# Strided sparse attention and a spectral mixer on one core: the last mode split by rows, the last Z in two tiles, the first U behind V

## The chip, the cores and the metric

The kernel runs on one core of a Trainium2 chip. The metric is the device time of one execution in microseconds (us), smaller is better. Runs of the same kernel differ by a few tenths of a per cent, so a time is a median of several.

## What is computed

Two stages follow each other, and nothing between them leaves the chip.

- Attention over q, k, v of shape (8 batches, 8 heads, 576 positions, 64): heads 0 to 3 look at the last 32 positions, heads 4 to 7 at the earlier positions of the same remainder modulo 32. The result x has 8 x 576 rows of 512.
- A spectral mixer: a Fourier transform of x along the positions, its first 64 modes multiplied by one complex 512 x 512 matrix each (w_r, w_i), the inverse transform y, then u = x + y and out = u + relu(u @ w_ch).

```python
X = np.fft.rfft(x, axis=1)
Xr, Xi = np.real(X[:, :64]), np.imag(X[:, :64])
Yr = einsum('bmd,mde->bme', Xr, w_r) - einsum('bmd,mde->bme', Xi, w_i)
Yi = einsum('bmd,mde->bme', Xr, w_i) + einsum('bmd,mde->bme', Xi, w_r)
u = x + np.fft.irfft(Y, n=576, axis=1)
return u + np.maximum(u @ w_ch, 0.0)
```

The mode matrices are 134 MB in float32. They are read once, turned into float16 on the way into SBUF.

## The kernel before, in words

**Order of the work.** The order of every engine's instructions is the order in which the program writes them (a manual schedule). Each engine works through its own list, and an instruction waits by semaphores for the tiles that it reads or overwrites. An instruction that waits holds up all that stands behind it on its engine.

**Stages.** Attention for the strided heads, then for the local heads, then what must be done with x before the inverse transform. Beside all of it the mode matrices stream in (w_fetch, from L157) and are multiplied (mode, from L614). The loads are issued on the POOL queue. A tile holds two modes, real part in partitions 0 to 63, imaginary part in 64 to 127. Most loads bring two modes (512 KB in float16); the last four modes are loaded one by one, two loads of 256 KB each (the list `single`, L189 and L190). A mode is needed for two halves of the 512 input columns; the second half of the modes 48 to 63 comes last (`rest`, L1036).

**The last modes.** For the second half, modes from 48 on are multiplied with the weights as the stationary operand: 16 small matmuls (L630), 4 output blocks e by 4 input chunks c, each with 16 columns moving. Eight modes share one PSUM tile y (L624). When the tile's modes are done, VectorE adds them to what the first half gave (spectrum, L563) and puts the sum into YT. In the last group that happens after mode 61 (six modes) and after mode 63 (two modes), both in the same y tile.

**V and U.** Since u @ w_ch and u are both linear in x and y, the kernel keeps for each block of 128 output rows a V part (x @ w_ch, what the relu will see) and a U part (x), and adds to both what the modes bring. Groups of 16 modes are added to the kept parts as soon as they are there (renew, L948; matmuls at L956 and L760; ScalarE writes V back at L251, VectorE adds U at L961). Only the last group of 16 modes is left for the end. For it the spectra are turned into Z = YT @ w_ch (spec_z, from L733, copied by ScalarE into zz) and YT turned around (transposes at L1051, copied by VectorE into yy at L1053). There are two sets of each, for batches 0 to 3 and 4 to 7.

**The output items.** 18 items of two blocks follow. For item k, v_early (L984) puts the kept V into a PSUM pair with an identity matmul (L987), new_rows (L994) adds the last modes' part from zz (L1001), ScalarE makes the relu (v_done, L1013); u_early (L989) and new_rows do the same for U from yy (L992, L1001); VectorE adds both (u_done, L1020) and SyncE stores (L1028). The loop (L1065) is one item deep: V of item k stands ahead of U of item k - 1. At k = 8 the second Z is computed into a tile `held` and copied by ScalarE, ahead of V 8.

**PSUM.** Eight banks: a pool p of three pairs (six banks), handed out in turn, and two y tiles. After mode 63 the y pool is closed; its two banks hold zp and yp, and after them the pair u.

**The end before the change**, in PE's order: mode 61; the last renew; mode 62; V 0, V 1, U 0 (the identity matmuls, into three p pairs); mode 63; Z; eight transposes; V rows of 0 and 1; U rows of 0; U 1 and its rows; then the loop.

Of the kernel before, what the change touches and what calls it, by code (L numbers as in the profile page):

```python
# [10 lines left out]
FP = mybir.dt.float32  # L11
# [5 lines left out]
S = 576  # L17
# [39 lines left out]
def kernel(  # L57
# [99 lines left out]
    def w_fetch(n=1):  # L157
        for _ in range(n):
            i = len(w_tiles)
            if i >= 2 * NM:  # L160
                return
            half, m = ORDER[i]
            if i // 2 in GUEST:
                wt = big.tile([128, 2, 4, DM], F16, tag=GUEST[i // 2], name="wt")
            else:
                wt = pw.tile([128, 2, 4, DM], F16, tag="w", name="wt")
            single = []
            for ri, src in enumerate((moe_w_r, moe_w_i)):
                dst = wt[ds(64 * ri, 64)]
                rows = src[m : m + 2, ds(256 * half, 256), :].rearrange(  # L170
                    "m (p c) e -> p m (c e)", c=4
                )
                dst = dst.rearrange("p m c e -> p m (c e)")


                ones = range(2)
                if ri and not m:
                    ones = [1]
                elif i in UNEVEN and not ri:
                    a = 0  # L180
                    for n in UNEVEN[i]:
                        nc.gpsimd.dma_start(dst[a : a + n], rows[a : a + n])
                        a += n
                    continue
                elif i < 2 * NM - 4:
                    nc.gpsimd.dma_start(dst, rows)  # L186
                    continue
                single += [(j, ri, dst[:, j], rows[:, j]) for j in ones]
            for _, _, to, rows in sorted(single, key=lambda x: x[:2]):  # L189
                nc.gpsimd.dma_start(to, rows)  # L190
            w_tiles.extend((wt[:, 0], wt[:, 1]))

# [57 lines left out]
    def act_copy(out, in_):  # L250
        nc.scalar.activation(out=out, in_=in_, func=ACTF.Copy)  # L251
# [362 lines left out]
    def mode(slot, m):  # L614
# [5 lines left out]
                mode_pair(slot, m - 1)  # L620
            return
        mi, mg = m % 8, m // 8
        if mi == 0:
            ypt[slot] = psum("y")  # L624
        yp = ypt[slot]
        yv = yp.rearrange("p (m e x) -> p m e x", m=8, e=4)
        wt = w_tiles[ORDER.index((half, m))]
        for e in range(4):
            for c in range(4):
                nc.tensor.matmul(  # L630
                    yv[:, mi, e, :],
                    wt[:, XC[c], ds(128 * e, 128)],
                    Xh[half][:, c, :, :, m],
                    start=(c == 0),
                    stop=(c == 3),
                )
        if m % 2:
            w_fetch()
        ends = {5: 6, 7: 2} if mg == 7 else {7: 8}
# [294 lines left out]
        if m >= 16 and m % 16 in (2, 4):  # L934
            spec(m // 16 - 1, m % 16 // 2 - 1)

    psum_pools(p=3)
    yctx = ctx.enter_context(ExitStack())
    pss["y"] = yctx.enter_context(tc.tile_pool(name="ps_y2", bufs=2, space=PSUM))

    def spec_late(mm, kept, eng):
        up = psum("p", pair=True)
        for bq in range(2):
            mm(2, bq, up[:, bq])
        for b in range(B):
            eng(kept[b][64:96], up[ds(32 * (b % 4), 32), b // 4])

    def renew(b, ts):  # L948
# [2 lines left out]
            v0, xo = v0s[b][:, ts[0] : ts[0] + 2], xos[b][:, ts[0] : ts[0] + 2]  # L951
        else:
            v0, xo = v0h[b // 2].unsqueeze(1), xoh[b // 2].unsqueeze(1)
        vp, up = psum("p", pair=True), psum("p", pair=True)
        for j, t in enumerate(ts):
            nc.tensor.matmul(vp[:, j], idn, v0[:, j], start=True, stop=False)  # L956
            rows_of(b, t, vp[:, j], zzs, False)
# [24 lines left out]
        return [kept[b][:, t] for b in bs] if t < 4 else [half[b // 2] for b in bs[::2]]  # L982

    def v_early(k):  # L984
        vps[k] = psum("p", pair=True)
        for j, r in enumerate(own(items[k], v0s, v0h)):
            nc.tensor.matmul(vps[k][:, j], idn, r, start=True, stop=False)  # L987

    def u_early(k):  # L989
        ups[k] = psum(("p", "u")[k % 2], pair=True)  # L990
        for j, r in enumerate(own(items[k], xos, xoh)):
            nc.tensor.matmul(ups[k][:, j], idn, r, start=True, stop=False)  # L992

    def new_rows(k, acc, spectra):  # L994
        bs, t = items[k]
# [38 lines left out]

    flush()
    rest = [(0, m) for m in range(SPLIT1, NM)] + [(1, m) for m in range(SPLIT0, NM)]  # L1036
    late[22] = [lambda: v_early(0), lambda: v_early(1), lambda: u_early(0)]
    for i, (slot, m) in enumerate(rest):
        mode(slot, m)
        for w in late.get(i, ()):  # L1040
            w()
    yctx.close()
    with tc.tile_pool(name="ps_s", bufs=1, space=PSUM) as pss["s"]:
        zp = pss["s"].tile([128, 512], FP, name="zp")
        yp = pss["s"].tile([128, 2, 512], F16, name="yp")
        spec_z(3, 0, zp)
        act_copy(zzs[0], zp)
        for bq in range(2):
            for e in range(4):
                lhs = YS["YT"][:, e, 3, ds(8 * bq, 8), :].rearrange("p x m -> p (x m)")  # L1050
                nc.tensor.transpose(yp[:, bq, ds(128 * e, 128)], lhs, idn)  # L1051
        for bq in range(2):
            nc.vector.tensor_copy(out=yys[bq], in_=yp[:, bq])  # L1053
    pss["u"] = pctx.enter_context(tc.tile_pool(name="ps_u", bufs=1, space=PSUM))

    for k in range(2):
        new_rows(k, vps[k], zzs)
    for k in range(2):
        v_done(k)
    for k in range(2):  # L1060
# [3 lines left out]
        u_done(k)  # L1064
    for k in range(2, LAST + 2):  # L1065
        if k == 8:
            held = psum("p", pair=True)[:, 0]
            spec_z(3, 1, held)
            act_copy(zzs[1], held)
        if k <= LAST:  # L1070
# [42 lines left out]
```

## Time and profile before

| what | value |
|---|---|
| three runs | 427.37, 427.93, 429.17 us; median 427.93 us |
| profiled execution, its span | 426.7 us, 1.2 us under the median of the runs |
| busy share of the span: PE, VectorE, ScalarE | 81%, 55%, 51% |
| loads on the POOL queue | 81.28 MB written, 96.2% of the time of 16 DMA engines |
| mode loads of 512 KB, issue to landing | 17.7 to 18.8 us |
| last mode load issued | 382.31 us |
| first store issued | 396.88 us |
| last store issued | 420.18 us |

The profile shows one execution on the chip. PE is TensorE's matmul, PEld its weight load, DVE VectorE, ACT ScalarE, POOL GpSimd, SP SyncE. L630 is line 630 of the kernel. The chain of work that ended last is followed back from the last instruction: at each step to what released it, or to the instruction before it on its engine. In the timeline, a row has its start, its duration, the engine, the line and the operation; for merged rows (x16) the duration is that of all; brackets give the idle time before it and what ended that. A matmul's duration includes its way through the array: 512 columns occupy PE for 0.216 us and end 0.38 us after their start. In rows for stretches, the columns are busy time of PE, PEld, DVE, ACT and POOL, then the clock granted to TensorE as a share of full speed, the busy share of the DMA engines and GB/s. The sum of busy time over all engines says little here; what counts is which wait ends last in the stretch around the change.

### The profile page before, as it was taken

To read this page: it belongs to the slowest core of one execution; us is meant where nothing else is said; L and a number is where in the kernel's file an instruction comes from. 1 tells how busy PE (TensorE), PEld (TensorE's weight loads), DVE (VectorE), ACT (ScalarE), POOL (GpSimd) and SP (SyncE) were. 2 spreads that over 40 slices of the span, in tenths; PEclk is the share of its full clock that TensorE was granted. 3 is DMA by queue.
4 is the path that set the end of the run, shared out by engine and by line. 5 is a ranking of instruction groups with operands and counts; after the bars stand their busy time and mean duration, and the time that the engine had idled before them with its cause. 6 is when DMAs were issued, how large, how long until landed. Compare 5 with 4: busy or idle time off the path is not lost.

```text
span 426.7 us, 9768 instructions
## 1 busy us (share of the span) xinstructions
PE 346.4 (81%) x4167; PEld 208.2 (49%) x4167; DVE 234.7 (55%) x466; ACT 218.3 (51%) x390; POOL 110.7 (26%) x196
## 2 busy tenths in 40 slices
PE   2977878769999698889768788878788867889993
PEld 2866767554656365566433344435444423445330
DVE  3788778851355154356113246746676354655884
ACT  1687678643656356556642235423442444443872
POOL 8332333322423222222222322222232222210000
PEclk9999899967999689999995889989999979989997
DMA  8999999999999999999999999999999999995698
GB/s 150 210 212 212 213 213 213 211 211 211 214 213 213 213 213 215 212 214 215 210 214 211 213 214 213 210 213 215 212 213 214 213 213 214 214 212 105 244 355 287
DMA packets 30938, 91.62 MB, mean 215 GB/s; under 512 B 4464, under 2 KB 5232, under 8 KB 30896
## 3 DMA queue, kind: packets, MB, share of 16 engines
q0 software_dynamic: 25168, 81.28, 96.2%
q1 hardware_dynamic: 4976, 9.13, 5.9%
q10 hardware_dynamic: 752, 0.61, 0.5%
q8 instruction: 32, 0.52, 0.5%
q14 instruction: 10, 0.08, 0.0%
HBM read 162.83 MB, written 9.44 MB: 404 GB/s over the span
## 4 chain that ended last, share of the span: by engine, by line
DMA 47%; PE 29%; DVE 14%; ACT 5%; issue 3%; DVEq 0%; POOL 0%; ACTq 0%; POOLq 0%
DMA wt<-in_moe_w_i_dram 38%; DMA wt<-in_moe_w_r_dram 7%; PE y L597 5%; DVE xb L241 3%; DVE kz L283 3%; PE p L987 2%; ACT X L251 2%; PE sc L532 2%; PE tp L413 2%; PE sc L459 1%; PE p L1001 1%; PE y L532 1%; PE p L760 1%; DVE yy L752 1%; DVE rec L240 1%
## 5 line engine op out<-in xcount | busy, mean ns | idle before, releaser
L597 PE MATMUL y<-wt,X 128*32 128x512 f16 (+1 forms) x448 | 70.9, 430 | 20.1 <-DMA wt<-in_moe_w_i_dram 20.1
L186 POOL DMA_DIRECT2D wt<-in_moe_w_r_dram x59 | 34.7, 588 | 126.4 <-PE y L597 56.3
L186 POOL DMA_DIRECT2D wt<-in_moe_w_i_dram x60 | 35.4, 590 | 68.3 <-DMA wt<-in_moe_w_i_dram 44.4
L597 PEld LDWEIGHTS <-X 128*32 128x32 f16 (+1 forms) x448 | 28.1, 140 | 39.4 <-DMA wt<-in_moe_w_i_dram 18.6
L727 DVE COPY xo<-tp 128x512 f16<-128x512 f16 x32 | 22.1, 691 | 36.8 <-PE tp L725 36.8
L726 ACT ACTIVATE v<-sc 128x512 f16<-128x512 f32 x32 | 19.1, 597 | 44.2 <-PE sc L717 44.2
L717 PE MATMUL sc<-w_cp,xT 128*128 128x512 f16 x128 | 36.9, 410 | 1.9 <-DVE xT L690 1.9
L489 ACT ACTIVATE PL<-sc 128x480 f16<-128x480 f32 (+1 forms) x48 | 27.0, 578 | 21.3 <-PE sc L475 21.0
L241 DVE TENSOR_TENSOR xb<-av,rec 90x256 f16<-90x256 f32 (+2 forms) x80 | 36.0, 450 | 2.8
L240 DVE RECIPROCAL rec<-av 90x4 f32<-90x4 f32 (+2 forms) x80 | 14.6, 183 | 39.3 <-PE av L504 28.2
L251 ACT ACTIVATE yr<-y 128x512 f16<-128x512 f32 x28 | 16.7, 597 | 36.8 <-PE y L597 35.6
L961 DVE TENSOR_TENSOR xo<-p,xo 128x1024 f16<-128x1024 f32 x16 | 19.6, 1225 | 21.7 <-PE p L760 21.7
L420 DVE COPY qT<-tp 128x576 f16<-128x576 f16 x16 | 11.9, 752 | 34.7 <-PE tp L413 34.7
L251 ACT ACTIVATE v<-p 128x1024 f16<-128x1024 f32 x16 | 16.4, 1023 | 23.1 <-PE p L760 23.1
L378 ACT ACTIVATE PL<-sc 90x360 f16<-90x360 f32 (+1 forms) x48 | 22.7, 490 | 7.0 <-PE sc L371 6.4
L251 ACT ACTIVATE v<-tp 128x640 f16<-128x640 f16 (+1 forms) x24 | 19.0, 807 | 11.8 <-PE tp L447 9.3
L413 PE MATMUL tp<-cI_s,ring 64*64 64x64 f16 x864 | 22.4, 197 | 2.7 <-DVE qT L420 2.4
L459 PE MATMUL sc<-cMl_s,cI_s 128*128 128x480 f16 (+1 forms) x48 | 19.4, 405 | 4.5 <-ACT PL L489 2.9
L276 PE MATMUL tp<-cI_s,ring 72*128 72x72 f16 x256 | 15.4, 207 | 8.7 <-DMA ring<-in_v_dram 7.1
L413 PEld LDWEIGHTS <-ring 64*64 64x64 f16 x864 | 17.5, 110 | 9.4 <-issue 5.4
L251 ACT ACTIVATE kz<-tp 64x360 f16<-64x360 f16 (+1 forms) x32 | 18.9, 592 | 6.2 <-PE tp L413 5.2
L1013 ACT ACTIVATE rl<-p 128x1024 f32<-128x1024 f32 (+1 forms) x19 | 18.4, 979 | 5.7 <-PE p L1001 3.1
(142 smaller groups left out, 737.9 us busy)
## 6 DMA issues: line engine op xcount, KB each, us to landing
wt<-in_moe_w_i_dram POOLq DMA_DIRECT2D x60, 512.0 KB, 18.8
wt<-in_moe_w_r_dram POOLq DMA_DIRECT2D x59, 512.0 KB, 17.7
out_dram<-osb SPq DMA_DIRECT2D x15, 512.0 KB, 3.4
ring<-in_v_dram POOLq DMA_DIRECT2D x8, 288.0 KB, 13.4
ring<-in_q_dram POOLq DMA_DIRECT2D x8, 288.0 KB, 13.6
ring<-in_k_dram POOLq DMA_DIRECT2D x8, 288.0 KB, 13.1
ring<-in_v_dram POOLq DMA_DIRECT2D x3, 512.0 KB, 14.8
ring<-in_q_dram POOLq DMA_DIRECT2D x3, 512.0 KB, 14.8
```

The lines of the kernel that those rows point to most:

```text
L186: nc.gpsimd.dma_start(dst, rows)
L241: nc.vector.tensor_tensor(out=dst, in0=val.rearrange("p h (q c) -> p h c q", c=4), in1=rec[0:n, 0:pieces] .to_broadcast((n, pieces, 64)) . ...
L251: nc.scalar.activation(out=out, in_=in_, func=ACTF.Copy)
L378: nc.scalar.activation(out=PS[0:n, ds(POFF[t], 4 * n)], in_=scp[0:n, 0 : 4 * n], func=ACTF.Exp, scale=SCALE,)
L413: nc.tensor.transpose(tp[ds(64 * hp, 64), ds(64 * i, 64)], qn[ds(64 * hp, 64), ds(64 * (9 * g + i), 64)], idn[ds(64 * hp, 64), ds(64 * hp, ...
L459: nc.tensor.matmul(scp[:, 0 : n * times].rearrange("p (h x) -> p h x", h=times), idn, mask_rows("cMl", n, times), start=True, stop=False,)
L489: nc.scalar.activation(out=dst, in_=src, func=ACTF.Exp, scale=SCALE)
L597: nc.tensor.matmul(yp[ds(a, 32), :], Xh[half][pr, c].rearrange("p b r (h m) -> p (b r h) m", h=2)[:, :, mm % 32], wt[pr, XC[c], :], start= ...
L717: nc.tensor.matmul(vp, xT[:, ch], w_chs["cp"][:, ch, :], start=(ch == 0), stop=(ch == 3),)
L726: nc.scalar.activation(out=v0, in_=vp, func=ACTF.Copy)
L727: nc.vector.tensor_copy(out=xo.rearrange("p (h q c) -> p h q c", h=2, c=4), in_=tp[:, 0:512].rearrange("p (h c q) -> p h q c", h=2, c=4),)
L961: nc.vector.tensor_tensor(out=xo, in0=up[:, 0:n], in1=xo, op=AluOp.add)
```

## The change

- The loads of mode 63 are cut in two by columns of the row (input chunks 0 and 1, then 2 and 3): four loads of 128 KB, in the order real, imaginary, real, imaginary. (w_fetch)
- Mode 62 opens a new y tile, so that modes 62 and 63 no longer share the tile of modes 56 to 61. Mode 63 begins with a matmul on a part of the constants that is zero (64 columns), then takes the eight steps on the first two chunks, two matmuls whose result is never read (warm(2), 512 columns each), then the other eight steps. (mode)
- The three p pairs get fixed names p0, p1, p2 in place of the turn (pair). Up to the last renew they go in turn. Then V takes p0 or p1 by the parity of the item (counted from where the turn ended), odd U and the unread matmuls p2, even U the pair u. `held` takes the pair of V of the same item.
- A third unread matmul stands between mode 63 and Z.
- The first Z is computed in two column halves into the two y tiles; ScalarE copies the first half, VectorE the second. The transposes go into p2 (as yp).
- U 0 no longer stands ahead of mode 63. It comes behind the V rows of items 0 and 1, in the pair u, and VectorE's copies of yp are written after it.

```diff
@@ -185,8 +185,13 @@
                 elif i < 2 * NM - 4:
                     nc.gpsimd.dma_start(dst, rows)
                     continue
-                single += [(j, ri, dst[:, j], rows[:, j]) for j in ones]
-            for _, _, to, rows in sorted(single, key=lambda x: x[:2]):
+                for j in ones:
+                    n = 2 * DM if m + j == NM - 1 else 4 * DM
+                    for a in range(0, 4 * DM, n):
+                        single.append(
+                            (j, a, ri, dst[:, j, a : a + n], rows[:, j, a : a + n])
+                        )
+            for *_, to, rows in sorted(single, key=lambda x: x[:3]):
                 nc.gpsimd.dma_start(to, rows)
             w_tiles.extend((wt[:, 0], wt[:, 1]))
 
@@ -620,20 +625,32 @@
                 mode_pair(slot, m - 1)
             return
         mi, mg = m % 8, m // 8
-        if mi == 0:
+        if mi == 0 or m == NM - 2:
             ypt[slot] = psum("y")
         yp = ypt[slot]
         yv = yp.rearrange("p (m e x) -> p m e x", m=8, e=4)
         wt = w_tiles[ORDER.index((half, m))]
-        for e in range(4):
-            for c in range(4):
-                nc.tensor.matmul(
-                    yv[:, mi, e, :],
-                    wt[:, XC[c], ds(128 * e, 128)],
-                    Xh[half][:, c, :, :, m],
-                    start=(c == 0),
-                    stop=(c == 3),
-                )
+        last = m == NM - 1
+        steps = [(e, c) for e in range(4) for c in range(4)]
+        if last:
+            steps.sort(key=lambda x: XC[x[1]] // 2)
+            nc.tensor.matmul(
+                yv[:, mi, :, :],
+                idn,
+                cs["cT"][:, S:640].rearrange("p (e x) -> p e x", e=4),
+                start=True,
+                stop=False,
+            )
+        for i, (e, c) in enumerate(steps):
+            if last and i == 8:
+                warm(2)
+            nc.tensor.matmul(
+                yv[:, mi, e, :],
+                wt[:, XC[c], ds(128 * e, 128)],
+                Xh[half][:, c, :, :, m],
+                start=(c == 0 and not last),
+                stop=(i == 15 if last else c == 3),
+            )
         if m % 2:
             w_fetch()
         ends = {5: 6, 7: 2} if mg == 7 else {7: 8}
@@ -934,12 +951,20 @@
         if m >= 16 and m % 16 in (2, 4):
             spec(m // 16 - 1, m % 16 // 2 - 1)
 
-    psum_pools(p=3)
+    psum_pools(p=1)
+    npair = [0]
+
+    def pair(n=None):
+        if n is None:
+            n = npair[0] % 3
+            npair[0] += 1
+        return pss["p"].tile([128, 2, 512], FP, tag=f"p{n}", name="p")
+
     yctx = ctx.enter_context(ExitStack())
     pss["y"] = yctx.enter_context(tc.tile_pool(name="ps_y2", bufs=2, space=PSUM))
 
     def spec_late(mm, kept, eng):
-        up = psum("p", pair=True)
+        up = pair()
         for bq in range(2):
             mm(2, bq, up[:, bq])
         for b in range(B):
@@ -951,7 +976,7 @@
             v0, xo = v0s[b][:, ts[0] : ts[0] + 2], xos[b][:, ts[0] : ts[0] + 2]
         else:
             v0, xo = v0h[b // 2].unsqueeze(1), xoh[b // 2].unsqueeze(1)
-        vp, up = psum("p", pair=True), psum("p", pair=True)
+        vp, up = pair(), pair()
         for j, t in enumerate(ts):
             nc.tensor.matmul(vp[:, j], idn, v0[:, j], start=True, stop=False)
             rows_of(b, t, vp[:, j], zzs, False)
@@ -982,14 +1007,19 @@
         return [kept[b][:, t] for b in bs] if t < 4 else [half[b // 2] for b in bs[::2]]
 
     def v_early(k):
-        vps[k] = psum("p", pair=True)
+        vps[k] = pair((npair[0] + k % 2) % 3)
         for j, r in enumerate(own(items[k], v0s, v0h)):
             nc.tensor.matmul(vps[k][:, j], idn, r, start=True, stop=False)
 
     def u_early(k):
-        ups[k] = psum(("p", "u")[k % 2], pair=True)
+        ups[k] = pair((npair[0] + 2) % 3) if k % 2 else psum("u", pair=True)
         for j, r in enumerate(own(items[k], xos, xoh)):
             nc.tensor.matmul(ups[k][:, j], idn, r, start=True, stop=False)
+
+    def warm(n):
+        spare = pair((npair[0] + 2) % 3)
+        for _ in range(n):
+            nc.tensor.matmul(spare[:, 0], idn, v0h[0], start=True, stop=True)
 
     def new_rows(k, acc, spectra):
         bs, t = items[k]
@@ -1034,27 +1064,39 @@
 
     flush()
     rest = [(0, m) for m in range(SPLIT1, NM)] + [(1, m) for m in range(SPLIT0, NM)]
-    late[22] = [lambda: v_early(0), lambda: v_early(1), lambda: u_early(0)]
+    late[22] = [lambda: v_early(0), lambda: v_early(1)]
     for i, (slot, m) in enumerate(rest):
         mode(slot, m)
         for w in late.get(i, ()):
             w()
+    warm(1)
+    last_y = YS["YT"][:, :, 3].rearrange("p e x m -> p e (x m)")
+    zp = [psum("y"), psum("y")]
+    for j in range(2):
+        for e in range(4):
+            nc.tensor.matmul(
+                zp[j][:, 0:256],
+                last_y[:, e, 0:128],
+                w_chs["n"][:, e, ds(256 * j, 256)],
+                start=(e == 0),
+                stop=(e == 3),
+            )
+    act_copy(zzs[0][:, 0:256], zp[0][:, 0:256])
+    nc.vector.tensor_copy(out=zzs[0][:, 256:512], in_=zp[1][:, 0:256])
+    yp = pss["p"].tile([128, 2, 1024], F16, tag=f"p{(npair[0] + 2) % 3}", name="yp")
+    for bq in range(2):
+        for e in range(4):
+            nc.tensor.transpose(
+                yp[:, bq, ds(128 * e, 128)], last_y[:, e, ds(128 * bq, 128)], idn
+            )
     yctx.close()
-    with tc.tile_pool(name="ps_s", bufs=1, space=PSUM) as pss["s"]:
-        zp = pss["s"].tile([128, 512], FP, name="zp")
-        yp = pss["s"].tile([128, 2, 512], F16, name="yp")
-        spec_z(3, 0, zp)
-        act_copy(zzs[0], zp)
-        for bq in range(2):
-            for e in range(4):
-                lhs = YS["YT"][:, e, 3, ds(8 * bq, 8), :].rearrange("p x m -> p (x m)")
-                nc.tensor.transpose(yp[:, bq, ds(128 * e, 128)], lhs, idn)
-        for bq in range(2):
-            nc.vector.tensor_copy(out=yys[bq], in_=yp[:, bq])
     pss["u"] = pctx.enter_context(tc.tile_pool(name="ps_u", bufs=1, space=PSUM))
 
     for k in range(2):
         new_rows(k, vps[k], zzs)
+    u_early(0)
+    for bq in range(2):
+        nc.vector.tensor_copy(out=yys[bq], in_=yp[:, bq, 0:512])
     for k in range(2):
         v_done(k)
     for k in range(2):
@@ -1064,7 +1106,7 @@
         u_done(k)
     for k in range(2, LAST + 2):
         if k == 8:
-            held = psum("p", pair=True)[:, 0]
+            held = pair((npair[0] + k % 2) % 3)[:, 0]
             spec_z(3, 1, held)
             act_copy(zzs[1], held)
         if k <= LAST:
```

## The prediction

> **What bounds the kernel now.** I read the chain of work that ended last first, then the timeline of its last 40 us, then stretches of a tenth of a microsecond around the last weights. Up to 377 us the chain is weight loads, one behind the other, with a DMA share above 1. From 377.2 us on TensorE (PE) has more queued than the loads hold back, so the rest of the span is a queue of PE passes with a few waits in it. All that the change touches lies there. The chain (start, duration, both in us):
>
> ```profile
> 388.80 0.50 DVE xo L961
> 389.30 0.64 issue
> 389.94 0.56 DVE YT L563
> 390.54 0.64 PE y L630 x16
> 391.17 0.86 PE p L987 x4
> 392.04 0.43 PE p L992 x2
> 392.47 0.49 PE y L630 x16
> 392.98 0.30 DVE YT L563
> 393.33 1.05 PE zp L736 x4
> 394.45 0.61 ACT zz L251
> 395.10 0.45 PE p L1001 x4
> 395.55 1.07 ACT rl L1013 x2
> 396.67 0.59 PE p L987 x2
> ...
> 404.18 1.01 ACT rl L1013
> 405.23 0.59 PE p L987 x2
> ```
>
> Mode 62 (L630, 390.54) waits for VectorE's add at L563, which stood behind the 1.23 us add of L961. Then four V passes, two U passes, mode 63, its add, Z (L736), ScalarE's copy, the V rows (L1001), the relu. From 396.67 the output items follow every 1.295 us (six streams of 512 columns at 0.216 us on PE), broken once: at 404.18 PE waits for a relu (item 7) before V of item 8. The timeline there (start, duration, engine, line, operation):
>
> ```profile
> 404.05 1.04 PE L736 MATMUL p<-w_ch,YT 128*128 128x512 f16 x4
> 404.16 1.02 ACT L1013 ACTIVATE rl<-p 128x1024 f32<-128x1024 f32 x1 [0.27 <-PE p L1001]
> 405.13 0.60 ACT L251 ACTIVATE zz<-p 128x512 f16<-128x512 f32 x1
> ```
>
> ScalarE takes the relu and only then copies the second Z (405.13 to 405.73). That order decides a cost below. The last weights (stretch, its length, PE, PEld, DVE, ACT, POOL, granted clock, DMA share, GB/s):
>
> ```profile
> 391.30:391.40 0.10, 0.10 (x2) 0.03 (x1) 0.00 (x0) 0.00 (x0) 0.00 (x0) 1.00 0.20 41
> 391.60:391.70 0.10, 0.10 (x3) 0.04 (x1) 0.00 (x0) 0.00 (x0) 0.00 (x0) 1.00 0.01 0
> ```
>
> The last data packet is at 391.4 and what follows at 391.6 is a sliver, the completion: mode 63's weights are there at about 391.65, while PE came to mode 63 at 392.3. So the loads do not set the end; PE's queue does.
>
> **The change, part by part.**
>
> 1. Mode 62 gets its own y tile, and its wait for L563 goes. PE's last pass before it starts at 389.62 and mode 62's first weight load at 389.93, 0.31 later. The same form shows the same 0.31 at 381.10 to 381.41, so this is PE's own pace and not a late load. Mode 62 can start at 389.97 instead of 390.54: **-0.57**. Late next would be its own weights: by the landing above, less two loads of 1.2 us, they are there at about 389.2 (an estimate). Bounds: 0 if they land at 390.5, 0.6 at best. V's buffers are read by L961 until 390.03 and by ScalarE until 390.43; V comes at 390.44 and 390.87, so nothing new waits.
>
> 2. Between the V passes and mode 63 the two U passes go (-0.43). In come one 64-column pass on zeros (16 small passes take 0.48, so 0.03) and, after eight of the 16 steps, two unread passes of 512 columns (+0.43): **+0.03**. PE then comes to the second half of mode 63 at 389.97 + 0.47 + 0.86 + 0.03 + 0.24 + 0.43 = 392.00, after the landing at 391.65. Without the two passes it would come at 391.57, so 0.35 of their 0.43 is pure cost, and splitting mode 63 by rows hides nothing that was waited for. Were the landing later than 392.00, every microsecond would count one for one.
>
> 3. Mode 63's two loads become four of half the row. POOL issues two more (0.52 us each) long ahead: the last issue was at 382.31, nine microseconds before its landing. Only these last loads stand behind them on POOL's queue. Rows of 2 KB in place of 4 KB: in 90 to 105 us, where the loads have rows of 2.3 KB, 211 GB/s moved, against 213 in 125 to 145 with 4 KB rows. I take 0. Bounds: 0, and twice the time per byte of mode 63's 512 KB, +2.5 us of landing, of which 0.35 is free. [...]
>
> 4. Z by halves. Before: add's end 393.28, Z 393.33, copy 394.45 to 395.05, V rows 395.10: 1.82 us. After: eight 256-column passes at half of 0.216, the last starting 0.76 after the first and ending 0.28 later (0.17 over its stream, as in the rows of 16, 128 and 512 columns); VectorE copies the second half (256 columns from PSUM, add row at L563: 0.42; ScalarE's row for 256 is 0.38 and starts earlier). 0.05 + 0.76 + 0.28 + 0.04 + 0.42 + 0.05 = 1.60: **-0.22**. Bounds: if a 256-column pass cost as much as one of 512 (seven starts of 0.216 and 0.38), +0.63; if the copy took 0.29, the 128-column row, -0.35. The third unread pass (0.22) lies in the 0.39 that PE waits for the add: 0. The transposes take 0.43 of the 0.5 that PE waits for the copies: 0.
>
> 5. U of item 0 goes behind the V rows: PE has 1.57 us there between V rows and the next V (it waits for the relu), and U 0, its rows, U 1 and its rows need seven streams of 0.216 = 1.51. **0**, with 0.06 to spare. Its rows need the yy copies, now behind the zz copy on VectorE: 0.38 after it, before U's passes end; U 1 takes the tile that both copies read, free 0.76 after, reached 0.87 after.
>
> 6. The fixed buffers. "held" (second Z, item 8) now takes the very buffer that V of item 8 takes next. Before, V 8 waited for relu 7 (405.18, PE at 405.23); now it waits for the copy of the second Z, behind that relu, ending at 405.73. In the built order V 8's wait on ScalarE stays and the V rows of item 8, which used to wait for zz, wait for nothing any more: V 8 already did. U 7 and all rows stand behind V 8 on PE. PE at 405.78: **+0.55**, on the path, since PE paces every later item. Bounds: 0 if V 8 does not wait, 0.85 if the whole gap after Z is lost.
>
> Sum: -0.57 + 0.03 - 0.22 + 0 + 0.55 = -0.21 us, from a span of 426.7 to 426.5. The three runs have their median at 427.93, 1.2 above that span; I put the same change on it: **427.7 us**.
>
> **The clock.** The unread passes are to keep PE busy, so the clock has to be looked at (same columns):
>
> ```profile
> 376.00:377.00 1.00, 0.00 (x0) 0.00 (x0) 1.00 (x2) 0.62 (x1) 0.00 (x0) 1.00 1.12 225
> 378.00:379.00 1.00, 1.00 (x4) 0.35 (x3) 0.00 (x0) 0.00 (x0) 0.00 (x0) 0.50 1.06 213
> 381.00:382.00 1.00, 1.00 (x21) 0.59 (x18) 1.00 (x2) 0.60 (x1) 0.00 (x0) 1.00 1.11 221
> 390.00:396.00 6.00, 4.79 (x60) 2.83 (x58) 2.13 (x6) 1.50 (x3) 0.00 (x0) 1.00 0.03 5
> ```
>
> After an idle stretch of 1.24 us (376.0 to 377.24) PE ran at half speed for some 3.5 us (a 512-column pass at 0.43). In 390 to 396 it idled 1.2 us in pieces of at most 0.5, and the clock stayed at 1.00. So the passes have no loss to prevent there: gain 0. [...]
>
> **Rivals.**
> - The stall at item 8 does not come (PE reaches V 8 late, or the copy is early). Speaks for it: nothing but slack I have not seen; against it, the built order. Then -0.21 - 0.55 = -0.76: 427.2 us.
> - The front gain is swallowed: mode 62 or mode 63's second half waits for its weights after all. With PE at full clock from 377 on, which the row at 378 shows to be a matter of one gap, PE would be up to 1.7 us earlier and the landing would bind in both kernels. Left are Z's gain and the stall: -0.22 + 0.55 = +0.33: 428.3 us.
> - **Slower.** The longer wait at item 8 (0.85 us of idle PE against 0.32) halves the clock as at 377. Decides from a gap near 1.2 us; price: 3.5 us at half speed, 1.75 us of lost work. -0.21 + 1.75 = +1.5: 429.5 us. Against it: 0.85 is below 1.24, and a gap of 1.15 us before 367.42 left the passes at 0.22.
> - The loads get worse by splitting, at the upper bound of part 3: -0.21 + 2.5 - 0.35 = +1.9: 429.9 us.
>
> **How the numbers follow.** Forecast 0.62, no stall 0.12, swallowed 0.16, clock 0.06, loads 0.04. Half a per cent, about what a measurement of this kernel can tell from no change, is 2.1 us. All five cases lie inside it; each has the spread of the runs shown (0.6 below and 1.2 above the median) on top, which takes some of the last two above it and little of the second below. So faster 0.03, within 0.90, slower 0.07. The range runs from the second case less 0.7 to the clock case without its spread: 426.5 to 429.4.
>
> **What would show it.** Mode 62 starting 0.3 after the pass before it, with no wait for L563; mode 63's second half starting right after the unread passes; 1.6 us from the last YT add to the V rows; the item period still 1.295; at item 8 PE waiting for the zz copy and starting V 0.05 after it, 3.0 us after V of item 7, and V 9 then without a wait. Wrong if the second half of mode 63 waits for a load, if the copies in two engines take over 0.5, if V 8 starts before the zz copy ends, or if a row of the last 35 us shows a clock under 1.00.

## The result, and the profile after

| | before | after |
|---|---|---|
| median of 22 runs each | 427.94 us | 429.21 us |
| lowest and highest of after | | 428.31 to 430.25 us |
| ratio, 95% interval | | 1.0029, 1.0022 to 1.0035 |
| median span, and time outside it (time less span) | 426.3 and 1.8 us | 426.7 and 2.4 us |

The change costs 1.27 us, 0.3%. The forecast was 427.7, 0.2 us of gain. The time lies inside the range of 426.5 to 429.4, but on the other side of the time before. About 0.4 to 0.5 us of it is in the span and 0.6 behind its end. (The span of before and its outside time come from 29 runs made beside the first experiments; the runs of before beside the later ones have median spans of 426.3 and 426.05.) One of the 22 runs of before took 459.45 us, in a slower state, and is left out of the ratio.

The chain of waits of the kernel after, from the last weights to V of item 8 (start, duration, both in us, what). In the line numbers of after, L647 is a step of a mode, L568 VectorE's add into YT, L1077 Z, L1085 and L256 the copies into zz, L1031 the rows, L1017 U, L1012 V and L1043 the relu:

```profile
391.33 0.14 issue
391.47 0.41 PE y L647 x8
...
391.90 0.30 DVE YT L568
...
392.25 1.06 PE y L1077 x8
...
393.33 0.44 DVE zz L1085
...
393.82 0.40 PE p L1031 x4
394.21 0.54 PE u L1017 x2
...
395.93 0.54 PE p L1012 x2
...
403.32 1.00 ACT rl L1043
404.33 0.55 ACT zz L256
404.88 0.04 issue
404.92 0.59 PE p L1012 x2
```

The profile of before that the prediction used had a span of 426.7, above the median of its kernel; the kernel before was run and profiled again (before_again, below), with a span of 425.9, a little under it. The same stretch of its chain:

```profile
391.25 0.14 issue
391.38 0.65 PE y L630 x16
...
392.06 0.30 DVE YT L563
...
392.40 1.05 PE zp L736 x4
...
393.53 0.61 ACT zz L251
...
394.18 0.45 PE p L1001 x4
394.62 1.07 ACT rl L1013 x2
...
395.74 0.59 PE p L987 x2
...
403.25 1.01 ACT rl L1013
404.26 0.04 issue
404.30 0.59 PE p L987 x2
```

Take both from the landing of the last weights, 391.33 and 391.25.

- Landing to V rows (L1031, L1001): 2.49 after, 2.93 before, a gain of 0.44.
- V rows to V of item 2 (L1012 at about 395.86 by the timeline, L987 at 395.74): 2.04 after, 1.56 before, a loss of 0.48.
- V of item 2 to V of item 8: 9.06 and 8.56, a loss of 0.50. In the first chain ScalarE's copy zz stands between the relu and V 8; in the second it does not.

So the front gains what the next stretch gives back, and the stall of item 8 is left: 0.5 us. The rest is not in any chain. The page of both kernels counts the same 32 packets, of 16 KB each, inside the span on one queue, of the kind that the page calls instruction (queue, kind: packets, MB, share of 16 engines):

```profile
q8 instruction: 32, 0.52, 0.5%
```

From 426 us on, behind the last instruction, the trace of after has one more:

```profile
q8 instruction: 1, 0.02, 1.0%
```

and that of before_again has none:

```profile
DMA packets 0, 0.00 MB, mean 0 GB/s; under 512 B 0, under 2 KB 0, under 8 KB 0
```

### The profile page after: what moved, and what is told of

It reads as the page before. It is cut to its first block, busy times and chain, and to the rows that moved or that the text cites. A ratio compares the mean times of both kernels' runs of the same rounds, so it can differ in the third digit from the quotient of the medians.

```text
span 426.4 us, 9788 instructions
## 1 busy us (share of the span) xinstructions
PE 345.1 (81%) x4175; PEld 207.7 (49%) x4175; DVE 235.3 (55%) x467; ACT 218.2 (51%) x390; POOL 112.1 (26%) x198
## 4 chain that ended last, share of the span: by engine, by line
DMA 56%; PE 22%; DVE 12%; ACT 4%; issue 3%; POOL 1%; DVEq 0%; POOLq 0%
DMA wt<-in_moe_w_i_dram 40%; DMA wt<-in_moe_w_r_dram 10%; DMA ring<-in_v_dram 4%; PE y L602 3%; DVE xb L246 3%; DVE kz L288 2%; PE p L1012 2%; PE sc L537 2%; ACT X L256 2%; PE p L1031 1%; DMA ring<-in_q_dram 1%; DVE yy L769 1%; DVE rec L245 1%; PE sc L734 1%; PE p L777 1%
## 5 line engine op out<-in xcount | busy, mean ns | idle before, releaser
L602 PE MATMUL y<-wt,X 128*32 128x512 f16 (+1 forms) x448 | 69.0, 420 | 20.9 <-DMA wt<-in_moe_w_i_dram 20.9
L256 ACT ACTIVATE yr<-y 128x512 f16<-128x512 f32 x28 | 16.7, 597 | 34.9 <-PE y L602 33.7
L256 ACT ACTIVATE v<-p 128x1024 f16<-128x1024 f32 x16 | 16.4, 1024 | 20.9 <-PE p L777 20.9
L256 ACT ACTIVATE v<-tp 128x640 f16<-128x640 f16 (+1 forms) x24 | 19.0, 807 | 12.1 <-PE tp L452 9.2
L256 ACT ACTIVATE kz<-tp 64x360 f16<-64x360 f16 (+1 forms) x32 | 19.0, 594 | 6.0 <-PE tp L418 5.0
L1043 ACT ACTIVATE rl<-p 128x1024 f32<-128x1024 f32 (+1 forms) x19 | 18.4, 979 | 7.1 <-PE p L1031 4.9
```

The costliest lines, as they stand in the source:

```text
L602: nc.tensor.matmul(yp[ds(a, 32), :], Xh[half][pr, c].rearrange("p b r (h m) -> p (b r h) m", h=2)[:, :, mm % 32], wt[pr, XC[c], :], start= ...
```

## The experiments

"Outside" is time less span. TensorE's instructions are counted in the program, matmuls and weight loads together (8381 before, 8398 after).

| kernel | TensorE instr. | median us | ratio to before, 95% | runs | span | outside: median, range |
|---|---|---|---|---|---|---|
| after | 8398 | 429.21 | 1.0029 (1.0022 to 1.0035) | 22 | 426.7 | 2.42, 1.75 to 3.28 |
| before_again | 8381 | 427.71 | 0.9994 (0.9983 to 1.0004) | 12 | 425.9 | 1.79 |
| before_split | 8382 | 428.01 | 1.0003 (0.9993 to 1.0012) | 12 | 426.2 | 1.79 |
| loads_whole | 8391 | 429.71 | 1.0052 (1.0032 to 1.0072) | 6 | 427.8 | 1.92, 1.78 to 3.01 |
| rows_only | 8382 | 427.66 | 0.9991 (0.9978 to 1.0004) | 12 | 425.85 | 1.79, 1.73 to 1.82 |
| halves_only | 8389 | 428.41 | 1.0007 (0.9993 to 1.0021) | 12 | 426.3 | 1.98, 1.74 to 3.23 |
| rows_and_halves | 8390 | 428.39 | 1.0012 (0.9999 to 1.0024) | 12 | 426.2 | 1.95, 1.85 to 3.29 |
| before_u_late | 8381 | 428.44 | 1.0008 (1.0000 to 1.0017) | 12 | 426.65 | 1.78 |
| held_apart | 8398 | 428.23 | 1.0006 (0.9995 to 1.0017) | 12 | 426.0 | 2.04, 1.74 to 3.1 |
| before_padded | 8399 | 428.24 | 1.0007 (0.9996 to 1.0019) | 12 | 426.3 | 1.92, four at 2.68 to 2.79 |
| after_short | 8378 | 428.19 | 1.0009 (1.0001 to 1.0018) | 11 | 426.4 | 1.79, 1.73 to 1.85 |
| held_short | 8378 | 428.03 | 0.9998 (0.9987 to 1.0009) | 12 | 426.2 | 1.81, 1.76 to 1.85 |
| no_passes | 8392 | 430.25 | 1.0054 (1.0042 to 1.0066) | 5 | 428.1 | 1.93, 1.75 to 3.26 |

Each ratio is to runs of before on the same chip beside it; the medians of those runs varied by some 0.3 us (427.80 to 428.1) between the three times that experiments were made.

### The kernel before, once more (before_again)

No edit.

> The kernel before, once more, for a second profile and for the spans beside the times. Theory A (the loss lies in the tail, and the profile of before was an execution slower than the median: time less span is the same for both kernels, about 2.4 us, as the after run with 428.84 us and a span of 426.4 shows): median about 428.0 us with spans about 425.6, and in the profile TensorE at full clock around 380 us, the last weights landing before 391 us. Rival B (the change costs outside the span, for example by a larger program): spans about 426.7 at a median of 428.0, so time less span about 1.3.

The time is the same. Of the expectations, the full clock at 380 us came; the rest of theory A did not (the outside time is 1.79 and not 2.4, and the last weights land at 391.25), and of rival B only that after has more time outside. The trace is not that of the prediction. Mode 62 and mode 63 in PE's timeline (start, duration, engine, line, operation, idle time before it and what ended that):

```profile
388.95 0.64 PE L630 MATMUL y<-X,wt 128*128 128x16 f16 x16 [0.67 <-DMA wt<-in_moe_w_i_dram]
...
391.38 0.64 PE L630 MATMUL y<-X,wt 128*128 128x16 f16 x16 [0.50 <-DMA wt<-in_moe_w_i_dram]
```

Both modes wait for their weights; neither waits for VectorE's add at L563. What differs ahead of them is the clock (stretch, length, PE, PEld, DVE, ACT, POOL, granted clock, DMA share, GB/s):

```profile
378.00:379.00 1.00, 1.00 (x6) 0.28 (x5) 0.42 (x1) 0.85 (x1) 0.00 (x0) 1.00 1.04 209
```

The profile of before had 0.50 in the same stretch. There PE came out of it late and had a queue in front of the last weights. All 14 profiles of this document agree. Four have the drop of the clock from about 377.6 to 381 (before, halves_only, loads_whole, held_short), and in none of them does mode 62 wait for its weights; in the ten without it, after among them, it does, 0.23 to 1.16 us. The length of the wait before 377 does not decide it: PE had waited 1.30 us at 376.60 here and kept its clock, 1.24 us in the profile of before. That profile was of an execution some 0.5 us slower than the median: its span of 426.7 plus 1.79 outside makes 428.5 (an estimate, its own time is not on record), not the 427.93 that the prediction put beside it.

### The loads cut in two (before_split, loads_whole)

before_split cuts only the loads of mode 63 in the kernel before:

```diff
-                single += [(j, ri, dst[:, j], rows[:, j]) for j in ones]
...
+                    n = 2 * DM if m + j == NM - 1 else 4 * DM
```

> The kernel before with only the loads of mode 63 cut into four of 2 KB rows; its matmuls as before. Theory A: the last landing 0.8 us later and with it everything behind, about 428.7, ratio 1.0018. Rival C (rows of 2 KB cost nothing, or PE's queue and not the landing sets the end): 428.0, ratio 1.000.

Rows of 2 KB show no cost: 1.0003 (0.9993 to 1.0012), and the last weights land at 391.32, against 391.25 in before_again.

loads_whole takes the cut out of the change, and with it the zero pass and the two unread passes between the halves:

```diff
-                    n = 2 * DM if m + j == NM - 1 else 4 * DM
+                    n = 4 * DM
...
-        last = m == NM - 1
+        last = False
```

> The changed kernel with mode 63 loaded by two loads of 4 KB rows and multiplied in one go, without the zero pass and the two unread passes in it; all else as in the change. Theory A (2 KB rows land the last weights about 0.8 us later; the halves give back 0.25): 0.5 to 0.7 us faster than the change, so about 428.6, ratio to before 1.0015. Rival C (rows of 2 KB cost nothing; the loss is all behind the last landing): same as the change or slower, 429.2 to 429.5.

It is slower than expected: by 0.5 us over after in the medians, by 1.0 in the ratios, with a median span 1.1 longer. Two things were taken out together, so this run does not say which of them did it; its profiled execution had the shortest span of the six (426.9), with the drop at 377 and full clock from 390 to 400 us, so it does not show the loss. The runs without passes, below, make the passes the likelier part, but that is not shown.

### Rows alone, halves alone, both (rows_only, halves_only, rows_and_halves)

rows_only is the kernel before with mode 62's own y tile, the cut loads and mode 63 in two halves, the start flag only on its first matmul, and no zero pass:

```diff
+        if mi == 0 or m == NM - 2:
...
+            steps.sort(key=lambda x: XC[x[1]] // 2)
...
+                start=(i == 0 if last else c == 0),
+                stop=(i == 15 if last else c == 3),
```

> The kernel before with the first third of the change alone: mode 62 opens its own y tile, mode 63's loads are cut by rows and its steps go in two halves; U of item 0 stays ahead of mode 63 and no unread pass is added (8382 TensorE instructions against 8381). Theory A (in a usual execution mode 63 waits for its weights, so only the steps behind the landing are saved): eight steps in place of sixteen behind the landing, -0.2 us, ratio 0.9995, landing to start of Z 0.2 shorter. The prediction's own reading (TensorE's queue sets the end, mode 62 starts 0.57 earlier): -0.55, ratio 0.9987. Time outside the span 1.8 in nearly all runs, as before.

427.66 against 427.80, the interval from 0.22% faster to 0.04% slower. Its chain has eight steps (0.41) behind the landing in place of sixteen (0.65), and mode 62 still waits 0.95 us for its weights. The theory that only these 0.24 us are saved fits; the prediction's own 0.55 (0.9987) lies within the interval too, but has no place in this trace.

halves_only puts Z by halves into the kernel before, in two banks, the transposes into the bank of the first half:

```diff
+        zp = [pss["s"].tile([128, 512], FP, tag=f"z{j}", name="zp") for j in range(2)]
...
+        act_copy(zzs[0][:, 0:256], zp[0][:, 0:256])
+        nc.vector.tensor_copy(out=zzs[0][:, 256:512], in_=zp[1][:, 0:256])
+        yp = pss["s"].tile([128, 2, 512], F16, tag="z0", name="yp")
```

> The kernel before with Z of the first four batches by column halves alone (two banks, ScalarE copies one half, VectorE the other), all else as before; 8389 TensorE instructions. Both theories: -0.2 us of span, 1.6 from the end of the last YT add to the V rows in place of 1.82, ratio 0.9995. Theory E (a program longer by some instructions fetches one more piece after the span in part of its executions): time outside the span 1.8 in most runs, about 2.7 in up to a third of them, so the median may keep the gain and the mean lose it; without E all runs at 1.8.

> Both gains together, U of item 0 ahead of mode 63, no unread pass, held as before; 8390 TensorE instructions. Theory A: span -0.4 to -0.45 against before, 425.9; time 427.6 to 427.8, ratio 0.999, if the time outside the span stays at 1.8 (theory E: in up to a third of the runs 0.9 more). By the prediction's terms it would be -0.57 - 0.22 = -0.8, ratio 0.998. If U of item 0 in that place is what keeps the clock up, no stretch at half speed between 390 and 400 us without any unread pass.

Both medians miss; the interval of halves_only still holds the expected 0.9995, that of rows_and_halves does not hold 0.999. The timeline of halves_only shows why it has no gain:

```profile
393.88 0.38 ACT L251 ACTIVATE zz<-zp 128x256 f16<-128x256 f32 x1 [3.60 <-PE zp L1048]
...
394.26 0.42 DVE L1056 CAST zz<-zp 128x256 f16<-128x256 f32 x1 [1.14 <-PE zp L1048]
394.31 0.61 PE L1061 MATMUL yp<-cI_s,YT 128*128 128x128 f16 x8
...
394.85 0.40 PE L1001 MATMUL p<-zz,cFl_s 32*128 32x512 f16 x4
394.96 0.76 DVE L1063 COPY yy<-yp 128x512 f16<-128x512 f16 x2 [0.27 <-PE yp L1061]
```

The transposes wait for ScalarE's copy to free their bank and then stand ahead of the V rows, which start 1.73 behind the add's end and not 1.6, and the copies yy come behind them, so V of item 2 starts 3.50 us after the add's end against 3.38 in before_again. So this does not measure the halves; it shows that they need a bank of their own for the transposes. With U 0 in a p pair ahead of mode 63 none is left; in the change the transposes take the pair that moving U 0 sets free. The two edits hang together, which the prediction did not weigh. The outside time of the two kernels reaches 3.2 and 3.3 us. The theory of the longer program had expected more time outside in up to a third of the runs; in rows_and_halves no run is under 1.85. In the profile of rows_and_halves the last weights landed at 392.64, over a microsecond later than in after or before_again, which is why its span (427.0) is above its median.

### U of item 0 behind the V rows (before_u_late)

```diff
-    late[22] = [lambda: v_early(0), lambda: v_early(1), lambda: u_early(0)]
+    late[22] = [lambda: v_early(0), lambda: v_early(1)]
...
+    u_early(0)
```

> The kernel before with the two U passes of item 0 moved behind the V rows of items 0 and 1, nothing else; same number of instructions. Theory A (behind the V rows they stand on the path, because each turn between passes of 128 and of 32 rows costs 0.1 us and the group then lasts 2.04 us instead of 1.57): 0.45 us slower less what mode 63 gains, which is nothing since it waits for its weights: 428.4, ratio 1.001. Rival G (as predicted: they lie beside the relu): 428.0, ratio 1.000; the V of item 2 still 1.57 us after the V rows of item 0.

The V rows and V of item 2 in its timeline:

```profile
394.47 0.40 PE L1001 MATMUL p<-zz,cFl_s 32*128 32x512 f16 x4 [0.29 <-ACT zz L251]
...
396.52 0.60 PE L987 MATMUL p<-v,cI_s 128*128 128x512 f16 x2
```

That is 2.05 us, as in after, against 1.56 in before_again. The time is 0.3 us longer (0 to 0.7). What PE does in that stretch, in the timeline of after:

```profile
393.82 0.40 PE L1031 MATMUL p<-zz,cFl_s 32*128 32x512 f16 x4
...
394.14 0.60 PE L1017 MATMUL u<-xo,cI_s 128*128 128x512 f16 x2
...
394.68 0.39 PE L1031 MATMUL u<-yy,cFl_s 32*128 32x512 f16 x2
...
395.00 0.61 PE L1017 MATMUL p<-xo,cI_s 128*128 128x512 f16 x2
...
395.54 0.39 PE L1031 MATMUL p<-yy,cFl_s 32*128 32x512 f16 x2
...
395.86 0.60 PE L1012 MATMUL p<-v,cI_s 128*128 128x512 f16 x2
```

Starts are 0.32, 0.54, 0.32, 0.54 and 0.32 apart. Two passes of 512 columns over 128 rows take 0.43 where the next work has 128 rows too, and 0.54 here; passes over 32 rows run side by side, two or four in one stream of 0.216, and take 0.32. So each turn from one shape to the other costs 0.107. Seven streams make 1.51, five turns 0.53, together 2.04. A regular item, in the timeline of before_again, has two turns:

```profile
396.65 0.59 PE L987 MATMUL p<-v,cI_s 128*128 128x512 f16 x2
397.08 0.59 PE L992 MATMUL p<-xo,cI_s 128*128 128x512 f16 x2
397.61 0.39 PE L1001 MATMUL p<-zz,cFl_s 32*128 32x512 f16 x2
397.62 0.39 PE L1001 MATMUL p<-yy,cFl_s 32*128 32x512 f16 x2
397.94 0.60 PE L987 MATMUL p<-v,cI_s 128*128 128x512 f16 x2
```

The four 32-row passes share one stream (they start together and the next V comes 0.32 later). The period of 1.295 is five streams and two turns. The prediction had read it as six streams, which gives 1.296 too. Why a turn costs 0.107 is not shown.

### held in the other V buffer (held_apart)

```diff
-        vps[k] = pair((npair[0] + k % 2) % 3)
+        vps[k] = pair((npair[0] + (k + (k >= 8)) % 2) % 3)
```

> The changed kernel with V's two buffers swapped from item 8 on, so that the second Z no longer sits in the buffer that V of item 8 takes. Theory A: PE starts V of item 8 behind relu 7 and not behind the copy of the second Z, 0.55 us earlier, and the time falls by that to about 428.65, ratio 1.0016. Rival D (the stores or VectorE pace the items, so that a stall of PE is caught up): no change in time, 429.2.

V of item 8 in after, and then in held_apart:

```profile
404.28 0.60 ACT L256 ACTIVATE zz<-p 128x512 f16<-128x512 f32 x1
404.92 0.59 PE L1012 MATMUL p<-v,cI_s 128*128 128x512 f16 x2 [0.69 <-ACT zz L256]
```

```profile
404.36 0.60 ACT L256 ACTIVATE zz<-p 128x512 f16<-128x512 f32 x1
404.47 0.59 PE L1012 MATMUL p<-v,cI_s 128*128 128x512 f16 x2
```

In after V 8 starts 0.04 behind the end of the copy; in held_apart it starts while the copy runs, with no wait for it, as in the kernel before. From V of item 2 (395.86 and 395.95) it comes after 9.06 and 8.52. The span's median falls by 0.7, and the ratio from 1.0029 to 1.0006, more than the 0.55 expected: the stall of 0.5 us is shown by the chain; the rest of that drop is within the intervals.

### The time outside the span (before_padded, after_short, held_short)

before_padded adds nine unread matmuls of 16 columns to the kernel before, far ahead of the end:

```diff
+        if b == 0 and ts[0] == 0:
+            for _ in range(9):
+                nc.tensor.matmul(vp[:, 0, 0:16], idn, v0[:, 0, 0:16], start=True, stop=True)
```

> The kernel before with nine unread 16-column matmuls more in the first renew of the last stage, where TensorE waits for weights anyway: 18 instructions more on TensorE, 8399 against 8381, about as many as the change has (8398). Theory E (the longer TensorE program costs at its end: the trace of the change shows a 33rd program fetch of 16 KB after the span, and time less span is 2.4 us at the median there, 1.8 before): span as before, time less span 2.0 to 2.5 us, so about 428.5, ratio 1.0015. Rival F (the time outside the span belongs to something else in the change): as before, time less span 1.8, ratio 1.000.

after_short takes ten matmuls out of the change, in modes that lie before the tail:

```diff
+        if half == 1 and m in (20, 22, 24, 26, 28):
+            steps = [x for x in steps if x[0] != 1]
```

> The changed kernel with ten matmuls (20 TensorE instructions) fewer: ten modes of the first half leave out one of their four input chunks, in a stretch where the weight loads set the pace, so the output is not the reference's. 8378 TensorE instructions. Theory E: time less span falls from 2.4 to 1.8 us at the same span, so about 428.6, ratio 1.0015. Rival F: nothing changes, 429.2, ratio 1.003.

held_short has this and the swap of held_apart.

> The change with two of its costs taken away together: held in the other V buffer, and ten matmuls fewer in ten modes of the first half (it leaves out one of their input chunks' terms in those modes; 8378 TensorE instructions), so that the last program fetch of the kernel before is the last here too. If the two costs add up (held 0.5 in the span, program 0.6 outside): span 426.0, time outside 1.8 in all runs, time 427.8 to 427.9, ratio 0.9995, which leaves U behind V (+0.47) against the gains of rows and halves (-0.45). If the fetch outside the span hangs on something else than the program's length: time outside 2.0 to 2.7 in part of the runs.

Removing twenty instructions brings the outside time back to a median of 1.79, with all 11 runs at 1.85 or less, and to 1.81 in held_short, where the same holds for all 12. (The time of after_short, 428.19, lies below the expected 428.6 because the median of its spans is 0.3 lower too; their means differ by 0.15.) Adding eighteen to the kernel before lifts it by 0.9 us in four runs of twelve, too few to show in the time (1.0007, 0.9996 to 1.0019). Over all kernels the line is sharp: no median over 1.81 with up to 8382 instructions, none under 1.92 with 8389 or more. That a longer TensorE program costs time behind the span is shown; that the cost is the fetch of one more 16 KB piece is a reading, which the profiled executions support in part: the three that show the packet behind the span (after, held_apart, rows_and_halves; all of 8390 instructions or more) lie 2.44, 3.10 and 1.96 outside, the ten others whose time is on record lie at 1.73 to 2.07, so the third tells nothing. Nor do the traces say that this queue is TensorE's. Why it strikes some executions and not others, and after more often (nearly all of 22 runs above 1.85) than before_padded, stays open. So does why the line lies between 8382 and 8389, and no run here tests whether such a fetch costs anything inside the span.

With both costs gone held_short is at 0.9998: what is left of the change, the gains in the front and U behind V, adds up to nothing, as the chain's 0.44 and 0.48 say.

Its profile has the drop of the clock at 377, as that of before has, and so shows the new order of the last modes where PE's queue binds and not the loads (L649 is a step of a mode):

```profile
389.49 0.38 PE L779 MATMUL p<-yy,cFs_s 96*64 96x512 f16 x2
...
389.80 0.65 PE L649 MATMUL y<-X,wt 128*128 128x16 f16 x16
...
391.90 0.40 PE L649 MATMUL y<-X,wt 128*128 128x16 f16 x8
```

Neither mode waits. Mode 62 starts 0.31 behind the pass before it, and the second half of mode 63 comes right behind the two unread passes. From that pass to the start of mode 63's add takes 2.84 us (389.49 to 392.33), against 3.36 in the profile of before (389.62 to 392.98): 0.52 less, in one execution each.

### The unread passes (no_passes)

```diff
-            if last and i == 8:
-                warm(2)
...
-    warm(1)
```

> The changed kernel without the three unread passes; 8392 TensorE instructions. Theory A (TensorE waits for the last weights in any case, so the passes cost nothing there and the clock does not need them): span as the change, 426.7; time lower only by what the six instructions fewer save behind the span, 0 to 0.6: 428.6 to 429.2. Rival H (the passes hold the clock up): spans 1 to 2 us longer, with a granted clock of 0.5 in a row behind 391 us.

Without its passes the change is slower by another microsecond (1.0054 against 1.0029), in the span: theory A missed, rival H came. Two stretches of its profile, the last before the Z and the one with it:

```profile
389.60:393.00 3.40, 2.19 (x38) 1.55 (x39) 0.75 (x2) 0.00 (x0) 0.00 (x0) 1.00 0.25 45
393.00:396.40 3.40, 3.40 (x21) 2.17 (x22) 1.11 (x3) 0.53 (x2) 0.00 (x0) 0.51 0.00 0
```

The clock falls to half for 3.4 us at 393.0 and Z takes 1.86 us in place of 1.06, though PE's longest single wait there was 0.73 us. In after the clock stays at 1.00 from 360.7 to 422.1 us, here around Z:

```profile
391.30:394.70 3.40, 2.99 (x33) 1.81 (x33) 1.47 (x4) 0.84 (x2) 0.00 (x0) 1.00 0.00 0
```

So taking the passes out costs the microsecond. That it is the clock rests on this one profile; one of the five runs has a span of 426.7, as after has. What the clock goes by is not shown. PE's busy share alone does not decide. rows_and_halves, with U 0 ahead of mode 63 and no passes, had less before its Z and kept its clock:

```profile
390.90:394.30 3.40, 2.00 (x26) 1.46 (x25) 0.29 (x1) 0.05 (x1) 0.00 (x0) 1.00 0.02 4
394.30:397.70 3.40, 3.13 (x25) 1.16 (x23) 2.48 (x6) 2.34 (x4) 0.00 (x0) 1.00 0.00 0
```

Nor is it the U passes in that place. before_u_late has neither them nor the unread passes ahead of mode 63, waited up to 0.93 us there, and kept its clock in its profile, in the next stretch too; its median span is 0.4 us above that of before, which is no more than the turns cost:

```profile
390.53:393.95 3.42, 2.10 (x28) 1.33 (x28) 0.29 (x1) 0.13 (x1) 0.00 (x0) 1.00 0.02 4
```

## Why the prediction was wrong, point by point

Three terms of its sum failed. The time outside the span was taken as unchanged without a reason, and grew by 0.6 us. U behind V (part 5) was put at 0 and cost 0.48. The front (parts 1 and 2) was put at -0.54 and brought -0.24, because the loads and not PE's queue hold up the last modes in after. The other terms were sized right.

- **The base.** The median of the runs was put beside the span of one profiled execution, which made an outside time of 1.2 us. It was 1.8, and the span was long. What was worked out from "the loads do not set the end; PE's queue does" belongs to an execution with a drop of the clock at 377. A rival named the other case ("the front gain is swallowed") and got a chance of 0.16; it is the case in after and before_again, and mode 62 waits for its weights in ten of the 14 profiles.
- **Part 1, -0.57:** the gain is not there in after. Mode 62 waits 1.16 us for weights in after and 0.67 in before_again. Where PE's queue does bind, in held_short, parts 1 and 2 bring 0.52 of their 0.54: the step was right for its base, and the base was not the usual one.
- **Part 2, "hides nothing that was waited for":** wrong for the same reason. The second half of mode 63 waits 0.35 for its load in after, so cutting by rows saves the 0.24 of eight steps, and the unread passes lie in waits.
- **Part 3, loads 0:** right (before_split).
- **Part 4, Z -0.22:** right. From the add's end to the V rows after takes 1.62 (392.20 to 393.82) against 1.82 (392.36 to 394.18). The term is read from the traces alone; halves_only could not isolate it.
- **Part 5, U behind V "0, with 0.06 to spare":** failed. Seven streams were right, five turns of 0.107 were missing: +0.48.
- **Part 6, held +0.55:** right, 0.50 by the chains, by the very wait that was named.
- **Outside the span, "the same change":** failed, and the largest miss: 0.6 us more, which no step considered. TensorE's longer program brings it; by what mechanism stays open.
- **The clock, "gain 0":** nothing in after contradicts it, since the passes are there; without them it costs a microsecond. The prediction went by the length of single waits: those of at most 0.5 us were safe. no_passes had at most 0.73 and lost the clock, before_u_late had 0.93 and kept it, so the length of a wait does not say.

The sum, from the traces: rows -0.24, Z -0.20, U +0.48, held +0.50, outside +0.6, together +1.1 of the measured 1.27. What is missing lies within the noise of the runs.

Of the rivals, the swallowed front gain came. The stall came as forecast; no clock drop came at item 8; the split loads cost nothing that shows. What made the kernel slower beyond that rival's 428.3 was U behind V and the program's length, which no rival had.

## What to carry to other kernels

Before a profile is taken as the base of tenths of a microsecond, set its span and outside time against the runs and look for a dip of the granted clock: what binds just behind the dip may not bind in the next execution. Count turns between matmul shapes as well as streams, and test a price per item on an irregular stretch, since a regular period can fit a wrong count as well as the right one. And in a tail that is already full, look at what a gain needs in instructions and shared buffers: both were paid for here (0.6 us behind the span, 0.50 us at item 8), and of the parts that were tried alone only the cut of mode 63 by rows came out ahead of the kernel before (427.66 against 427.80), and its interval still holds no change.

## What the runs showed of the hardware

- A turn between 128-row and 32-row matmuls costs 0.107 us on PE (two U passes take 0.54 us ahead of 32-row passes in after, 0.43 us from V to U in before_again); four 32-row passes of 512 columns share one stream (in before_again they start at 397.61 and 397.62, and the next V at 397.94).
- The clock's drops last about 3.4 us or a multiple (3.4 at 393.0 in no_passes, 6.8 at 346.8 in before) and begin behind a thin stretch, not at a gap: in the 3.41 us ahead of each drop PE was busy for 0.64 to 2.37 us in before and 0.23 to 2.33 us in after, and the drop at 377.55 in before begins 0.31 us after the wait of 1.24 us had ended. In the traces of before and after all drops begin whole multiples of 3.413 us apart (in before, those at 346.83 and 377.55 are nine apart; in no_passes, those at 358.90 and 393.04 are ten apart), from a start that differs from execution to execution (357.27 in after and 358.90 in no_passes are 1.63 us apart, no multiple of it). How much work keeps the clock at full speed is not settled here (2.19 us of 3.4 lost it in no_passes, 2.00 kept it in rows_and_halves).
- With 8389 or more instructions in TensorE's program (8382 or fewer do not), these kernels lose between nothing and 1.5 us behind the span (outside times of 1.74 to 3.29 us, against a median of 1.79 in before_again).
- The last weights landed anywhere between 391.25 us (before_again) and 392.64 us (rows_and_halves) in executions of nearly the same loads, so a single profile says little about a tenth of a microsecond there.
